# A fused attention and feed-forward kernel on one core: tile 0's late layernorm on ScalarE, mask work on GpSimd in pieces, and phi_q@KV of four tiles in pairs

## The chip, the core and the metric

The kernel runs on one core of a Trainium2 chip. The core has TensorE (PE in the profile: matmuls, and PEld, its weight loads), VectorE (DVE), ScalarE (ACT), GpSimd (POOL) and SyncE (SP, which here only issues DMAs), each with a queue of its own that it works through in order; they wait for each other through semaphores. Matmuls write to PSUM, which has eight banks. The metric is the device time of one execution in microseconds; times below are microseconds unless marked otherwise.

## What is computed

For one sequence of 2048 rows of 640 numbers, all in bf16:

```
x  = A_x;  n = layernorm(x)
q, k, v = split(n @ wqkv)                       # 32 heads of 20
pq, pk = q @ w_phi[h], k @ w_phi[h]             # per head, 20 x 20
phi_q = [softmax(pq), softmax(-pq)]             # over the 20; phi_k alike
kv = phi_k^T @ v;  z = sum over rows of phi_k   # per head
h  = x + (phi_q @ kv / (phi_q . z + 1e-6)) @ wo
m  = layernorm(h)
out = h + (gelu(m @ w_gate) * (m @ w_up)) @ w_down     # 1536 inner
```

## The kernel before

The 2048 rows are 16 tiles of 128 rows (t = 0 to 15), four of them a block (b = 0 to 3). The 640 columns are five chunks of 128. The order of every engine's queue is the order in which the code issues instructions (`manual_schedule`), written out by hand.

**First stage, lines 411 to 505.** For each tile: layernorm statistics, the normalized tile transposed into `LN1T` (by PE for tiles 0 to 5, by a transposing DMA on SP's queue for the rest), v and k by matmul (k with w_phi folded into the weights), `E` = exp of k with both signs on ACT (L310), their sums per head `sk` on DVE (L317), reciprocals `rs` (L321), and `vt` = v times `rs` for both signs (L325): sign 1 always on POOL, sign 0 on POOL for the tiles in `VP` (0, 2, 4, 6, 9, 11) and on DVE for the others, where it is issued one tile later, between `sk` and `rs` of the next tile. `kv_tile` (L343) sums phi_k^T v of all tiles in one PSUM tile, `kvp`; the last tiles run at the end of the stage, after the first chunks of q. Tiles 0 and 1 go through k and v without their row scale, which is applied later, so their true layernorm must be written into `LN1T` before block 0's q: at t == 10 DVE applies it to tile 0 (`ln_ap(0)`, L144) and to tile 1 (`ln_a(1)`, L390), and SP transposes both. At t == 9, POOL clears `KV` and makes the 0/1 mask `kmask` (two memsets, four affine_selects, two copies into `KV`, L489 to L497). At t == 13 SP issues the loads of `Wg`, `Wo` and `Wu`.

**q.** Chunks of phi_q are numbered 5 b + c, and `QG` groups them in the order in which they run; the first four groups run at t == 15, the rest in the list at lines 739 to 781, with the attention of tiles 0 and 1 between them.

**Second stage: attention of a tile, and the feed-forward.** `attn_a` computes phi_q@KV (`ab`, L546: 20 matmuls on half the rows of the array each) and copies it to `AB` in SBUF; `attn_b` takes denominators on POOL (`pr`, `den`), `attn_b2` their reciprocal `rd` on DVE and the weights `w` on POOL, `attn_b3` the products `tt` and the sum `o` on DVE and a DMA transpose into `oT`; `attn_c` multiplies by wo (`po`); `attn_d` adds x on DVE with the row sum as a by-product (L633, L636); `attn_d2` takes the sum of squares on ACT (`sq`) and five or six tiny POOL instructions (L651 to L657) for the scale; `attn_e` applies the layernorm on ACT (`ln`, L139) and transposes it by DMA into `LN2T`. The feed-forward has units: `gate_up` (`gu`: ten matmuls into two halves, gelu `g` on ACT, product `GT` on DVE) for each of 12 inner chunks f, and `down` (`pd`: 12 matmuls for half of a tile's columns, then `y` on DVE and a store). `weave` runs a list of units and issues, ahead of unit i, the attention steps numbered up to i:

```
weave(gus(0, 0, 256) + downs(0, (0, 1)), ...)      # tiles 0, 1: 16 units
weave(gus(0, 256, 512) + downs(0, (2, 3)), ...)    # tiles 2, 3: 16 units
weave(gus(1, 0, 512) + downs(1, range(4)), ...)    # block 1, then 2 and 3
```

A step's number is that of its tile plus an offset from a tuple (`SHORT`, `SHORT2`, `LONG`), and steps beyond the list's end go over to the next one. Up to `split()`, PSUM is four tiles of two banks (`gtile`), where a gelu waits for both halves of its `gu`; after it, eight single banks (`bank`), where it waits for its own half. `attn_a` copies a tile's `ab` with two ACT copies; `attn_pair`, only after the split, runs two tiles' `ab` back to back into eight banks and gives half of the eight copies to ACT and half to DVE (L559). In before, tiles 8 and 9, 10 and 11, 12 and 13, 14 and 15 are pairs; tiles 2 to 7 are singles.

Of the kernel before, what the change touches and what calls it, by code (L numbers as in the profile page):

```python
# [10 lines left out]
ALU = mybir.AluOpType  # L11
# [6 lines left out]
def kernel(  # L18
# [12 lines left out]
    nc = tc.nc  # L31
# [17 lines left out]
    LQ = (7, 8, 9, 9, 10)  # L49
    FQ = (10, 11, 12, 13, 14)  # L50

    QG = ((0, 1), (2, 3), (4, 5), (6,), (7, 8), (9, 10), (11, 12), (13, 14), (15,), (16,), (17,), (18,), (19,))
    QT = (15, 15, 15, 15)
    T3 = 3

# [20 lines left out]
    x_sb = [const.tile([P, 4, D], BF16, name=f"x_sb{b}") for b in range(NB)]  # L76
# [5 lines left out]

    Eq = [const.tile([P, len(g), 2, 512], BF16, name=f"Eq{j}") for j, g in enumerate(QG)]
    ident = const.tile([P, P], BF16, name="ident")
# [6 lines left out]
    def eq(t, c, s):  # L91
        for E, g in zip(Eq, QG):
            if t // 4 * NC + c in g:
                return E[:, g.index(t // 4 * NC + c), s, t % 4 * P:(t % 4 + 1) * P]

    def small(pool, shape, name, bufs=3):
        return pool.tile(shape, F32, name=name, bufs=bufs)

    def gtile(name):
        return psG.tile([P, 2, 512], F32, name=name, tag="G")  # L100

    def ln_stats(pool, tiles, tag, act=True, between=None, log=False):

        n = len(tiles)
        mv = small(pool, [P, n, nc.vector.BN_AGGR_DIM], "mv" + tag)
        stats = small(pool, [P, n, 2, nc.vector.BN_STATS_DIM], "stats" + tag)
        for j, xt in enumerate(tiles):
            for i in range(2):
                nc.vector.bn_stats(stats[:, j, i, :], xt[:, i * HD:(i + 1) * HD])
                if between and i == j == 0:  # L110
                    between()
        for j in range(n):
            nc.vector.bn_aggr(mv[:, j, :], stats[:, j])
        ve = small(pool, [P, n], "ve" + tag)
        rstd = small(pool, [P, n], "rstd" + tag)
        if log is not False:

            def root():
                nc.scalar.activation(ve, mv[:, :, 1], ACTF.Ln, bias=eps)
                nc.scalar.activation(rstd, ve, ACTF.Exp, scale=-0.5)  # L120

            if log is True:
                root()
            else:
                log.append(root)
        else:
            nc.gpsimd.tensor_scalar_add(ve, mv[:, :, 1], EPS)
            nc.gpsimd.tensor_tensor(rstd, ve, nhalf[:, 0:n], op=ALU.pow)

        mr = small(pool, [P, n], "mr" + tag)  # L130
        if act:
            for j in range(n):
                nc.gpsimd.tensor_scalar(mr[:, j:j + 1], mv[:, j, 0:1], rstd[:, j:j + 1], -1.0,
                                        op0=ALU.mult, op1=ALU.mult)
        return [(xt, mv[:, j, 0:1], rstd[:, j:j + 1], mr[:, j:j + 1]) for j, xt in enumerate(tiles)]
# [11 lines left out]
    def transpose_to(dst, src, on_pe, on_dve=False):  # L147

        if on_pe:
            tp = psG.tile([P, 16, P], BF16, name="tp", tag="G")  # L150
            for c in range(NC):
                nc.tensor.transpose(tp[:, c, :], src[:, c * P:(c + 1) * P], ident)  # L152
            (nc.vector.tensor_copy if on_dve else nc.scalar.copy)(dst, tp[:, 0:NC, :])  # L153
        else:
            nc.sync.dma_start_transpose(dst, src)
# [7 lines left out]
    p1 = p1_cm.__enter__()  # L163
# [81 lines left out]
    lnp, Ek, Vt = {}, {}, {}  # L245

    CT = (0, 1)
    nrstd = [p1.tile([P, 1], F32, name=f"nrstd{t}") for t in CT]

    def ln_0(t):  # L250
        xt, mean, rstd, _ = lnp[t] = ln_stats(p1, [x_sb[0][:, t, :]], f"c{t}", False, None, True)[0]
        nc.gpsimd.tensor_scalar(nrstd[t], rstd, -1.0, None, op0=ALU.mult)
        xc = fp.tile([P, D], BF16, name="xc", bufs=2)
        nc.vector.tensor_scalar(xc, xt, mean, None, op0=ALU.subtract)
        return xc
# [5 lines left out]
    def ln_ap(t, on_act=False, on_pe=False):  # L261
        ln = (ln_act if on_act else ln_dve)(p1, "1", *lnp[t])
        if on_pe:
            lnp[t] = ln
        else:
            transpose_to(LN1T[t // 4][:, :, t % 4 * P:(t % 4 + 1) * P], ln, False)
# [92 lines left out]
    def q_mm(j, part=(0, 1)):  # L359

        if 0 in part:
            pqs[j] = gtile("pq")
        for i, bc in enumerate(QG[j]):
            if i not in part:
                continue
            b, c = divmod(bc, NC)
            for kc in range(NC):
                nc.tensor.matmul(pqs[j][:, i, :], lhsT=Wq2[:, kc, c * P:(c + 1) * P], rhs=LN1T[b][:, kc, :],  # L368
                                 start=(kc == 0), stop=(kc == NC - 1))

    def q_exp(j, signs=(0, 1)):
        for s in signs:
            nc.scalar.activation(Eq[j][:, :, s, :], pqs[j][:, 0:len(QG[j])], ACTF.Exp, scale=(1.0, -1.0)[s])  # L373

# [82 lines left out]
    for t in range(NT):  # L457
        if t == T3:
            ps_cm.close()
            psG = ps_cm.enter_context(tc.tile_pool(name="psG", bufs=3, space=PSUM, reuse_waits="tile"))  # L460
            psK = ps_cm.enter_context(tc.tile_pool(name="psK", bufs=1, space=PSUM, reuse_waits="tile"))
            kvp = psK.tile([P, 2, 512], F32, name="kvp")
        k_tile(t)
        if t == 0:
            ln_ap(6)
        if t in FQ:
            fold(WqT, Wq2, True, [i for i, f in enumerate(FQ) if f == t])
        for j in range(len(QT)):
            if t == QT[j]:
                q_mm(j)  # L470
                q_exp(j)
        for i in KVG.get(t, ()):
            kv_tile(i)
        if 0 < t < NT - 4:
            v_mm(t + 4)
        if t > 0 and t + 6 < NT:
            ln_ap(t + 6, on_act=True)
        if 0 < t < NT - 4:
            v_ev(t + 4)
        if t % 2 == 0 and t + 8 < NT:  # L480
            ln_st(t + 8, t + 9)
        k_norm(t)
        load_T(WqT, 0, *[i for i, f in enumerate(LQ) if f == t])
        if t == 10:

            ln_ap(0)
            transpose_to(LN1T[0][:, :, P:2 * P], ln_a(1), False)
        if t == 9:
            nc.gpsimd.memset(KV, 0.0)  # L489
            nc.gpsimd.memset(kmask, 1.0)  # L490
            for r in HALF:
                nc.gpsimd.affine_select(out=kmask[r], in_=kmask[r], pattern=[[4, NC], [-Dh, 4]],
                                        compare_op=ALU.is_ge, fill=0.0, base=0, channel_multiplier=1)
                nc.gpsimd.affine_select(out=kmask[r], in_=kmask[r], pattern=[[-4, NC], [Dh, 4]],
                                        compare_op=ALU.is_ge, fill=0.0, base=Dh - 1, channel_multiplier=-1)
            nc.gpsimd.tensor_copy(KV[:, :, 0, :, KC - 1], kmask)
            nc.gpsimd.tensor_copy(KV[:, :, 1, :, 0], kmask)  # L497
        if t == 13:
            nc.sync.dma_start(Wg, wg_v)
            nc.sync.dma_start(Wo, wo_v)  # L500
            nc.sync.dma_start(Wu, wu_v)
# [60 lines left out]
    def attn_a(t, dve=0):  # L562
        attn_a_mm(t)
        AB, ab = ABs[t % 2], st[t, "ab"]
        for u in ((1, 0) if t in (5,) else (0, 1)):
            (nc.vector.tensor_copy if u >= 2 - dve else nc.scalar.copy)(
                AB[:, :, u * UH:(u + 1) * UH].rearrange("p s h f -> p s (h f)"), ab[u][:, :, 0:UH * KC])
        st[t] = AB
# [215 lines left out]
    def attn_at(t, i, offs):  # L784

        fns = (attn_a, attn_b, attn_b2, attn_b3, attn_c, attn_d, attn_d2, attn_e)
        return [(i + o, fn, t) for fn, o in zip(fns, offs) if o >= 0]

    SHORT = (0, 2, 3, 4, 9, 9, 10, 12)
    SHORT2 = (0, 2, 3, 4, 10, 10, 11, 13)  # L790
    LONG = (0, 1, 2, 5, 5, 6, 7)

    def attn_rest(t, i):
        return [(i + o, fn, t) for fn, o in zip((attn_b, attn_b2, attn_b3, attn_c, attn_d, attn_d2, attn_e), LONG)]

    weave(gus(0, 0, 256) + downs(0, (0, 1)),
          attn_at(2, 0, (-1, 0, 1, 2, 7, 7, 8, 10)) + attn_at(3, 1, (1, 2, 3, 4, 9, 9, 10, 12)) + attn_at(4, 6, SHORT2) + attn_at(5, 9, SHORT2) +
          attn_at(6, 13, SHORT2))  # L800
    weave(gus(0, 256, 512) + downs(0, (2, 3)),
          attn_at(7, 0, SHORT) + [(12, split), (14, attn_pair, 8), (16, attn_pair, 10)] + attn_rest(8, 15) +
          attn_rest(9, 17) + attn_rest(10, 19) + attn_rest(11, 21))
    weave(gus(1, 0, 512) + downs(1, range(4)),
          [(18, attn_pair, 12), (20, attn_pair, 14)] + attn_rest(12, 19) + attn_rest(13, 21) + attn_rest(14, 23) +
# [34 lines left out]
```

## Time and profile before

| what | before |
|---|---|
| time, median of 3 runs (lowest, highest) | 277.28 (276.76, 277.5) |
| the profiled execution's own time | 277.27 |
| its span, first to last instruction | 275.5 |
| PE busy in the span | 270.3 |
| granted TensorE clock | 1.000 |

The span by stages, with each engine's busy time (from the view that sums busy time in windows):

| stage | window | PE | DVE | ACT | POOL |
|---|---|---|---|---|---|
| start | 0 to 16.5 | 14.90 | 11.24 | 10.90 | 5.32 |
| k, v, first part | 16.5 to 46 | 29.50 | 28.99 | 27.10 | 24.95 |
| k, v, second part, first q | 46 to 70.2 | 23.49 | 22.34 | 18.55 | 15.69 |
| q, tiles 0 and 1 | 70.2 to 89.5 | 19.30 | 13.39 | 15.73 | 2.49 |
| first weave | 89.5 to 116.9 | 27.36 | 18.84 | 15.29 | 10.93 |
| second weave | 116.9 to 142.7 | 25.80 | 15.87 | 14.06 | 10.96 |
| the rest | 142.7 to 275.5 | 129.93 | 65.03 | 38.56 | 26.77 |

How to read it: PE's busy time fills nearly all of every stage after the start. A row of the profile's time order gives start, duration, engine, line of the code, operation, output and inputs with their shapes; "xN" merges N instructions, and brackets give the idle time before and what ended it. An instruction that waits inside the engine for something else than a semaphore shows this as a longer duration, not as idle time.

### The profile page before, as it was taken

The numbers are of one execution on the slowest core, as the hardware profiler recorded it, in microseconds if no ns is written. First come the engines' busy times: TensorE is split into PE (matmuls) and PEld (weight loads), VectorE is DVE, ScalarE is ACT, GpSimd is POOL, SyncE is SP. The second block draws the span as 40 slices with busy tenths as digits, with TensorE's granted clock in tenths as the row PEclk, the third lists the DMA queues.
The fourth block names the chain that finished last, engine by engine and source line by source line (L and its number), as shares of the span: only waits on it lengthen the run. The fifth ranks groups of instructions, "written<-read, shape, count | busy, mean of one in ns | idle before, by whom it ended". The sixth has DMA issues, their size and how long they took to land.

```text
span 275.5 us, 5939 instructions
## 1 busy us (share of the span) xinstructions
PE 270.3 (98%) x2345; PEld 173.6 (63%) x2345; DVE 175.7 (64%) x333; ACT 140.2 (51%) x241; POOL 97.1 (35%) x218
## 2 busy tenths in 40 slices
PE   7999999999899999999999999999999999999995
PEld 4777777765455887788764545675455576444574
DVE  5889999999495776675478773356866333333322
ACT  5789898869489755374552345223245510223100
POOL 4248897765202317365312553101165300000000
DMA  7963525589820021323111142110123111000011
GB/s 197 209 230 61 75 51 101 83 266 394 264 91 0 4 48 38 84 48 77 26 48 48 26 69 51 38 61 2 48 47 71 27 48 50 24 0 0 0 50 48
DMA packets 42235, 21.37 MB, mean 78 GB/s; under 512 B 35040, under 2 KB 40416, under 8 KB 42208
## 3 DMA queue, kind: packets, MB, share of 16 engines
q1 hardware_dynamic: 41552, 20.98, 30.1%
q8 instruction: 18, 0.29, 0.5%
q10 hardware_dynamic: 656, 0.03, 0.2%
q14 instruction: 9, 0.07, 0.1%
HBM read 10.18 MB, written 2.62 MB: 46 GB/s over the span
## 4 chain that ended last, share of the span: by engine, by line
PE 86%; issue 4%; DVE 4%; DMA 2%; ACT 1%; POOL 1%; SPq 0%; DVEq 0%; ACTq 0%; POOLq 0%
PE gu L678 37%; PE pd L697 19%; PE po L618 8%; PE pv L277 6%; PE pk L277 5%; PE pq L368 5%; PE ab L546 2%; DMA Wv<-in_A_wqkv_dram 2%; DVE sk L317 2%; DVE rs L321 1%; PE kvp L343 1%; PE tp L152 1%; POOL vt L325 1%; PE pv L293 1%; PE wa L232 1%
## 5 line engine op out<-in xcount | busy, mean ns | idle before, releaser
L681 ACT ACTIVATE g<-gu 128x512 bf16<-128x512 f32 (+1 forms) x60 | 30.7, 512 | 68.9 <-PE gu L678 68.7
L684 DVE TENSOR_TENSOR GT<-gu,g 128x512 bf16<-128x512 f32 (+1 forms) x60 | 34.5, 580 | 47.8 <-PE gu L678 39.2
L678 PE MATMUL gu<-LN2T,Wg 128*128 128x512 bf16 (+1 forms) x300 | 61.8, 337 | 0.0
L678 PE MATMUL gu<-LN2T,Wu 128*128 128x512 bf16 (+1 forms) x300 | 61.8, 337 | 0.0
L697 PE MATMUL pd<-Wd,GT 128*128 128x320 bf16 (+2 forms) x396 | 53.5, 295 | 0.0
L697 PEld LDWEIGHTS <-GT 128*128 128x128 bf16 x396 | 37.9, 98 | 14.7 <-DVE GT L684 0.2
L678 PEld LDWEIGHTS <-Wu 128*128 128x128 bf16 x300 | 29.4, 98 | 22.6
L678 PEld LDWEIGHTS <-Wg 128*128 128x128 bf16 x300 | 28.8, 98 | 21.4
L277 PEld LDWEIGHTS <-LN1T 128*128 128x128 bf16 x290 | 27.8, 98 | 10.5
L700 DVE TENSOR_TENSOR y<-pd,x_sb 128x320 bf16<-128x320 f32 (+2 forms) x29 | 13.9, 480 | 28.9 <-PE pd L697 28.9
L325 POOL TENSOR_TENSOR vt<-vS,rs 128x672 bf16<-128x672 bf16 x22 | 29.1, 1343 | 9.1 <-DVE rs L321 8.8
L618 PE MATMUL po<-Wo,oT 128*128 128x320 bf16 x160 | 24.3, 299 | 0.0
L277 PE MATMUL pk<-Wk,LN1T 128*128 128x320 bf16 x160 | 24.2, 299 | 0.0
L368 PE MATMUL pq<-LN1T,Wq 128*128 128x512 bf16 x100 | 23.1, 379 | 0.0
L317 DVE TENSOR_REDUCE sk<-E 128x64 f32<-128x1280 bf16 x16 | 22.9, 1430 | 0.0
L373 ACT ACTIVATE Eq<-pq 128x1024 bf16<-128x1024 f32 (+1 forms) x26 | 20.0, 830 | 1.7 <-PE pq L368 1.7
L618 PEld LDWEIGHTS <-oT 128*128 128x128 bf16 x160 | 15.6, 98 | 7.4 <-ACT oT L153 0.5
L310 ACT ACTIVATE E<-pk 128x640 bf16<-128x640 f32 x28 | 18.2, 707 | 3.8 <-PE pk L277 3.8
L277 PE MATMUL pv<-Wv,LN1T 128*128 128x320 bf16 x130 | 19.8, 299 | 0.0
L595 DVE TENSOR_TENSOR tt<-AB,w 128x1280 bf16<-128x1280 f32 x12 | 17.8, 1486 | 1.1 <-POOL w L588 0.9
L139 ACT ACTIVATE ln<-x_sb,v,rstd 128x640 bf16<-128x640 bf16 x14 | 12.9, 920 | 10.4 <-POOL v L657 10.0
L368 PEld LDWEIGHTS <-Wq 128*128 128x128 bf16 x100 | 9.4, 98 | 10.0
(114 smaller groups left out, 292.8 us busy)
## 6 DMA issues: line engine op xcount, KB each, us to landing
out_dram<-y SPq DMA_DIRECT2D x15, 160.0 KB, 1.8
Wg<-in_B_w_gate_dram SPq DMA_DIRECT2D x1, 1920.0 KB, 7.9
Wu<-in_B_w_up_dram SPq DMA_DIRECT2D x1, 1920.0 KB, 12.8
Wd<-in_B_w_down_dram SPq DMA_DIRECT2D x1, 1920.0 KB, 7.9
x_sb<-in_A_x_dram SPq DMA_DIRECT2D x2, 640.0 KB, 6.3
Wo<-in_A_wo_dram SPq DMA_DIRECT2D x1, 800.0 KB, 9.5
x_sb<-in_A_x_dram SPq DMA_DIRECT2D x4, 160.0 KB, 3.4
Wv<-in_A_wqkv_dram SPq DMA_DIRECT2D x2, 320.0 KB, 4.6
```

The costliest lines, as they stand in the source:

```text
L277: nc.tensor.matmul(ps[:, u, 0:HD], lhsT=lnT(t, c), rhs=W[:, c, u * HD:(u + 1) * HD], start=(c == 0), stop=(c == NC - 1))
L310: nc.scalar.activation(Ek[t][:, s, :].rearrange("p (u f) -> p u f", u=2), pk[:, :, 0:HD], ACTF.Exp, scale=((lnp[t][2], nrstd[t]) if t in C ...
L317: nc.vector.reduce_sum(sk, Ek[t].rearrange("p s (h f) -> p (s h) f", f=Dh), axis=AX.X)
L325: eng.tensor_tensor(vt[:, s], vS[t % 8], rs[:, s * H:(s + 1) * H, None].to_broadcast([P, H, VC]), ALU.mult)
L368: nc.tensor.matmul(pqs[j][:, i, :], lhsT=Wq2[:, kc, c * P:(c + 1) * P], rhs=LN1T[b][:, kc, :], start=(kc == 0), stop=(kc == NC - 1))
L373: nc.scalar.activation(Eq[j][:, :, s, :], pqs[j][:, 0:len(QG[j])], ACTF.Exp, scale=(1.0, -1.0)[s])
L595: nc.vector.tensor_tensor(tt.rearrange("p s (h f) -> p s h f", f=Dh), num, w[:, :, :, None].to_broadcast([P, 2, H, Dh]), ALU.mult)
L618: nc.tensor.matmul(pos[u], lhsT=st[t][:, c, :], rhs=Wo[:, c, u * HD:(u + 1) * HD], start=(c == 0), stop=(c == NC - 1))
L678: nc.tensor.matmul(gu[i][:, 0:n], lhsT=W[:, c, f * P:(f + 1) * P], rhs=LN2T[b][:, c, a0:a1], start=(c == 0), stop=(c == NC - 1))
L681: nc.scalar.activation(g[:, 0:n], gu[0][:, 0:n], ACTF.Gelu_apprx_tanh)
L684: nc.vector.tensor_tensor(st[b, "g", f][:, a0:a1], gu[1][:, 0:n], g[:, 0:n], ALU.mult)
L697: nc.tensor.matmul(ps, lhsT=st[b, "g", f][:, tl * P:(tl + 1) * P], rhs=Wd[:, f, f0:f1], start=(f == 0), stop=(f == NF - 1))
```

## The change

- `ln_ap(0)`, tile 0's late layernorm, goes from DVE at t == 10 to ACT at t == 12, ahead of E of tile 13 in ACT's queue; its transpose is issued behind that of tile 1. ACT's form needs minus mean times scale, so `ln_0` computes that for tile 0 with one more POOL instruction. Tile 1's (`ln_a(1)`) stays.
- POOL's mask work is cut in three: the memsets at t == 7, the affine_selects at t == 8, the copies into `KV` at t == 10, each behind that tile's `vt`.
- `QG`: chunks 5 and 6 (block 1) run first; 4 stands alone.
- Tile 3's steps move (offsets below); tile 4 to 7's `ab` become two pairs in the down units of the first weave, ahead of units 13 and 15, and `split()` moves from unit 12 of the second weave to unit 12 of the first. The other steps of tiles 4 to 7 follow at new offsets (`MID`), most of them in the second weave, and now use single banks (two L633 per tile in place of one L636, one more POOL instruction, L651).

Lines of the changed kernel are up to four higher (L678 becomes L682, L559 becomes L563).

```
-    QG = ((0, 1), (2, 3), (4, 5), (6,), (7, 8), ...
+    QG = ((5, 6), (0, 1), (2, 3), (4,), (7, 8), ...
...
-        xt, mean, rstd, _ = lnp[t] = ln_stats(...)[0]
+        xt, mean, rstd, mr = lnp[t] = ln_stats(...)[0]
         nc.gpsimd.tensor_scalar(nrstd[t], rstd, -1.0, None, op0=ALU.mult)
+        if t == 0:
+            nc.gpsimd.tensor_scalar(mr, mean, nrstd[0], None, op0=ALU.mult)
...
         if t == 10:
-
-            ln_ap(0)
             transpose_to(LN1T[0][:, :, P:2 * P], ln_a(1), False)
-        if t == 9:
+        if t == 12:
+            ln_ap(0, on_act=True)
+        if t == 7:
             nc.gpsimd.memset(KV, 0.0)
             nc.gpsimd.memset(kmask, 1.0)
+        if t == 8:
             for r in HALF:
                 nc.gpsimd.affine_select(out=kmask[r], ...)
                 nc.gpsimd.affine_select(out=kmask[r], ...)
+        if t == 10:
             nc.gpsimd.tensor_copy(KV[:, :, 0, :, KC - 1], kmask)
             nc.gpsimd.tensor_copy(KV[:, :, 1, :, 0], kmask)
...
-        for u in ((1, 0) if t in (5,) else (0, 1)):
+        for u in ((1, 0) if t in (4,) else (0, 1)):
...
-    SHORT = (0, 2, 3, 4, 9, 9, 10, 12)
-    SHORT2 = (0, 2, 3, 4, 10, 10, 11, 13)
+    MID = (0, 1, 2, 8, 8, 9, 11)
     LONG = (0, 1, 2, 5, 5, 6, 7)
-    def attn_rest(t, i):
-        return [(i + o, fn, t) for fn, o in zip((attn_b, attn_b2, attn_b3, attn_c, attn_d, attn_d2, attn_e), LONG)]
+    def attn_rest(t, i, offs=LONG):
+        return [(i + o, fn, t) for fn, o in zip((attn_b, attn_b2, attn_b3, attn_c, attn_d, attn_d2, attn_e), offs)]
...
     weave(gus(0, 0, 256) + downs(0, (0, 1)),
-          attn_at(2, 0, (-1, 0, 1, 2, 7, 7, 8, 10)) + attn_at(3, 1, (1, 2, 3, 4, 9, 9, 10, 12)) + attn_at(4, 6, SHORT2) + attn_at(5, 9, SHORT2) +
-          attn_at(6, 13, SHORT2))
+          attn_at(2, 0, (-1, 0, 1, 2, 7, 7, 8, 10)) + attn_at(3, 1, (2, 2, 3, 4, 8, 8, 9, 11)) +
+          [(12, split), (13, attn_pair, 4), (15, attn_pair, 6)] + attn_rest(4, 14, MID) + attn_rest(5, 16, MID) +
+          attn_rest(6, 18, MID) + attn_rest(7, 20, (0, 1, 2, 7, 7, 8, 10)))
     weave(gus(0, 256, 512) + downs(0, (2, 3)),
-          attn_at(7, 0, SHORT) + [(12, split), (14, attn_pair, 8), (16, attn_pair, 10)] + attn_rest(8, 15) +
+          [(14, attn_pair, 8), (16, attn_pair, 10)] + attn_rest(8, 15) +
           attn_rest(9, 17) + attn_rest(10, 19) + attn_rest(11, 21))
```

More of the change, by code (lines that the diff above doesn't have):

```diff
@@ L50 @@
     FQ = (10, 11, 12, 13, 14)
-    QG = ((0, 1), (2, 3), (4, 5), (6,), (7, 8), (9, 10), (11, 12), (13, 14), (15,), (16,), (17,), (18,), (19,))
+    QG = ((5, 6), (0, 1), (2, 3), (4,), (7, 8), (9, 10), (11, 12), (13, 14), (15,), (16,), (17,), (18,), (19,))
     QT = (15, 15, 15, 15)
@@ L250, in ln_0 @@
     def ln_0(t):
-        xt, mean, rstd, _ = lnp[t] = ln_stats(p1, [x_sb[0][:, t, :]], f"c{t}", False, None, True)[0]
+        xt, mean, rstd, mr = lnp[t] = ln_stats(p1, [x_sb[0][:, t, :]], f"c{t}", False, None, True)[0]
         nc.gpsimd.tensor_scalar(nrstd[t], rstd, -1.0, None, op0=ALU.mult)
+        if t == 0:
+            nc.gpsimd.tensor_scalar(mr, mean, nrstd[0], None, op0=ALU.mult)
         xc = fp.tile([P, D], BF16, name="xc", bufs=2)
```

## The prediction

> **What bounds the kernel now.** I read the page's header and busy times first, then the waits of PE, then the time order of each engine where PE waits or where the change touches it. All times are microseconds on the profile's clock.
>
> ```profile
> span 275.5 us, 5939 instructions
> PE 270.3 (98%) x2345; PEld 173.6 (63%) x2345; DVE 175.7 (64%) x333; ACT 140.2 (51%) x241; POOL 97.1 (35%) x218
> ```
> ```profile
> PE wu L214 <- PEq L824: 0.8, 1, 0.8
> PE kvp L343 <- POOL vt L325: 0.7, 1, 0.7
> PE pv L293 <- DMA Wv<-in_A_wqkv_dram: 0.5, 1, 0.5
> ```
> PE is busy 98% of the span at full clock, and its waits sum to 2.0. A gain must shorten PE's work or remove the one wait in the middle (kvp, at 69.87; the matmul before it started at 68.96, and 20 ns is the step there, so removing it gives at most 0.88). A loss is any new wait on PE, and there are many places for one.
>
> That wait ends a chain of DVE and POOL work from 46 on. The time order of DVE, then of POOL (start, duration):
> ```profile
> 51.53 1.81 DVE L144 TENSOR_SCALAR ln<-x_sb,mvc,rstdc 128x640 bf16<-128x640 bf16 x1
> 53.27 0.43 DVE L390 TENSOR_SCALAR ln<-x_sb,va 128x640 bf16<-128x640 bf16 x1
> 53.62 1.47 DVE L317 TENSOR_REDUCE sk<-E 128x64 f32<-128x1280 bf16 x1
> 55.01 1.72 DVE L325 TENSOR_TENSOR vt<-vS,rs 128x672 bf16<-128x672 bf16 x1
> ```
> ```profile
> 49.76 2.58 POOL L325 TENSOR_TENSOR vt<-vS,rs 128x672 bf16<-128x672 bf16 x2 [1.32 <-DVE rs L321]
> 52.28 0.83 POOL L489 MEMSET KV<- 128x880 bf16 x1
> ...
> 54.70 1.31 POOL L325 TENSOR_TENSOR vt<-vS,rs 128x672 bf16<-128x672 bf16 x1
> ```
> Tile 0's ln needs 0.43 (its neighbour's duration) and took 1.81: it ended 0.23 after POOL's memset. DVE's vt ended 0.72 after POOL's vt (56.01). So an elementwise instruction of DVE stands while POOL works, and here it stood through two POOL instructions in a row, vt and memset.
>
> **Part 1: ln(0) to ScalarE, mask work in pieces.** DVE loses L144. The other ln (tile 1, L390) stays in its place and is asked for at the same 51.53. POOL's vt of tile 9 still runs to 52.34; behind it now comes vt of tile 10 at once (its rs ended at 51.61), to 53.6. If DVE stands through both, as it did through vt and memset, L390 ends at 53.85 to 54.2, after the two small copies, and sk(11) starts 0.15 to 0.5 later than 53.62. But vt(10) of DVE then finds POOL idle: 0.85 instead of 1.72, the uncovered duration at 67.79. rs(11) comes 0.4 to 0.75 earlier than 56.65. The four mask instructions, now ahead of vt(9), can take 0.5 of that back. If DVE gets in after one POOL instruction, L390 ends at 52.6, rs(11) comes 2.0 earlier, and the whole 0.88 is gained. If the memset, now behind vt(7) of POOL, holds up DVE's vt(7), DVE loses 0.83 there and the stage ends up to 0.5 later. From rs(11) on both orders are equal. Between −0.5 and 0.88 I take a gain of **0.4**, the middle of the case that the row shows.
>
> The Trainium skill ("SBUF — State Buffer", Who interferes with whom) says that a DVE instruction with two SBUF inputs contends with GpSimd instructions that read SBUF, not with one that only writes, and that the lock goes to whoever issues first, for the whole instruction. By its first half the memset costs vt(7) nothing; by its second DVE should get in between two POOL instructions, the gain would be 0.88 and the sum 278.24. The row of 1.81 speaks against the second half.
>
> On ACT ln(0) costs 0.92 at 54.40; E(13) behind it ends at 56.4, and ACT was idle for 1.43 before 57.75, so PE's pk and wa find their banks free. Its transpose on SP starts near 55.4 and lands 2.6 later, at 58.0; Wg, Wo and Wu behind it are issued about 1 later and needed after 79. Chunks of block 0, which need it, come second (61.4) since chunks 5, 6 go first. The added product for tile 0 runs on POOL at 5.7, idle until 8.29. All this costs nothing; without the chunk order the margin would be 1.2 (59.23 against 58.0).
>
> **Part 2: pairs.** The chain of waits gives the price of phi_q@KV on PE:
> ```profile
> 97.48 0.50 PE ab L546 x20
> 97.97 1.20 PE gu L678 x10
> ...
> 137.49 0.94 PE ab L546 x40
> 138.42 3.37 PE pd L697 x24
> ```
> A single costs 0.50 and 0.11 in what follows (10 gu matmuls elsewhere take 1.09); a pair 0.94 and 0.11 (24 pd: 3.26). Four singles become two pairs: 4 x 0.61 − 2 x 1.05 = **0.34 saved**.
>
> The price is in the covers. I put the changed order on the old clock from tile 2's ab (89.56), with a gu unit at 1.09, a po at 1.36, a pd unit at 1.63. Without ab(4) in front, po(2) comes at 98.39 (was 99.01) and po(3) at 101.93 (was 104.25); their oT lands 2.6 after issue, at 98.45 and about 102.1. Waits: 0.1 and 0.15. Pair (4,5) starts near 108.4, and ACT's copies of it stand behind ln(3). Two views of the old pair (8,9) show how tight that is:
> ```profile
> 134.06 3.42 PE L697 MATMUL pd<-Wd,GT 128*128 128x320 bf16 x24
> 137.42 1.00 PE L546 MATMUL ab<-KV,Eq 64*128 64x88 bf16 x40
> 138.35 3.43 PE L697 MATMUL pd<-Wd,GT 128*128 128x320 bf16 x24
> ```
> ```profile
> 135.53 0.92 ACT L139 ACTIVATE ln<-x_sb,v,rstd 128x640 bf16<-128x640 bf16 x1 [0.82 <-POOL v L657]
> 137.82 1.52 ACT L559 COPY AB<-ab 128x352 f32<-128x352 f32 x4 [1.38 <-PE ab L546]
> ```
> The pair takes all eight PSUM banks; the next pd uses the bank that ACT's first copy frees, at 138.27, only 0.08 ahead. A later ACT is a later PE, one for one. For pair (4,5), ln(3) ends at about 109.1 where the copy wanted 108.8: 0.2. These three: **0.45 lost** (bounds 0 and 0.6).
>
> Then tiles 4 to 7 run their whole tail inside gus(0, 256, 512). Pair (6,7) starts at 112.50. DVE copies its half and reaches rd(4) 2.24 later (old: 141.72 to 143.96), 114.74, and tt(4) at 115.7. Steps from the old rows: tt to o 1.52, o to GT 0.41, GT to rd 0.36, rd to tt 0.95, together 3.24. So tt(5) 118.94, tt(6) 122.18, then o, GT, rd, GT (0.27), 0.36 and the two L633 of tile 4 (0.81): tt(7) at 125.91. DVE is saturated; po(4) was done at 123.09. Now POOL's statistics of tile 4 meet tt(7):
> ```profile
> 106.74 1.44 POOL L652 TENSOR_SCALAR v<-sm 128x1 f32<-128x1 f32 x1 [0.92 <-DVE x_sb L636]
> 108.26 0.38 POOL L653 TENSOR_SCALAR v<-v 128x1 f32<-128x1 f32 x1
> ```
> That is the same meeting in before (tt 106.55 to 108.04): 0.27 became 1.44, and the last of five POOL steps ended 3.47 after tt began, ln at 3.50. With one more step (L651, 0.29), ln(4) is at 129.70. ACT's order is ln(4), sq(5), ln(5), sq(6), ln(6), ln(7), copies of pair (8,9). ln to the next takes 0.83, sq to its ln 2.32 (1.00 to L654, then 0.35, 0.66, 0.27, 0.04): sq(5) 130.53, ln(5) 132.85, sq(6) 133.68, ln(6) 136.00. Tile 7's six POOL steps (2.28) wait for tile 6's: ln(7) 138.36, first copy 139.19. PE's sum from 112.50 (0.94, 1.74, twelve gu, four po, two pd) puts pair (8,9) at 136.97, so the copy is due at 137.37. It is 1.82 late, less 0.08: **1.74 lost**. Upward, POOL's pr may hold up each tt (0.13 three times: 2.1); downward, an undelayed ACT costs 0.
>
> PE finds its banks otherwise: the closest are po(5) (GT freed at 125.1, due 125.9), po(6) (128.2, 128.8) and tile 7's oT (130.5, 131.2). Queued behind ACT's wait are those copies, GT of unit 11 for the last pd matmul (0.2, inside the 1.74), and nothing on SP that is due. LN2T(7) lands near 142 and is due at 143.
>
> **Sum,** against the profiled execution's own 277.27 (span 275.5 and 1.77 around it; the median of the runs is 277.28): 277.27 − 0.40 − 0.34 + 0.45 + 1.74 = 278.72. Forecast **278.7**.
>
> **Rivals.** (a) Faster: the covers hold. If ln(7) starts by 136.5, ACT meets the copy, nothing is lost, and 277.27 − 0.88 − 0.34 = 276.05. For it: in before ACT idled 1.38 ahead of that copy, and tiles 8 to 11 go through the same order unharmed. Against: their units last 2.16, these 1.09, and DVE needs 4.4 per tile (3.24, a GT, two L633) where PE gives 3.5 (two gu, one po). It decides where the ln chain is 1.74 shorter. (b) No change: DVE and POOL do not meet at tt(7). Then sq(5) follows STT(5) at 129.4 and the copy is 0.65 late: 277.27 − 0.40 − 0.34 + 0.45 + 0.65 = 277.6. Likewise if (a)'s cover holds but Part 1 brings little: 277.0. (c) Worse: DVE falls 0.4 further behind, PE waits for GT too, and Part 1 turns into 0.5: 277.27 + 0.5 − 0.34 + 0.6 + 2.1 = 280.1. (d) Part 1 does not do what it says, since L390 now waits as long as both did: the 0.40 goes, 279.1, inside the forecast's range.
>
> **How the numbers follow.** Forecast with (d), 278.1 to 279.5: 0.50. (b), 276.5 to 278.1: 0.27. (a): 0.15. (c): 0.08. The range leaves out about half of (a) and most of (c): 276.2 to 279.8; the forecast's own is 278.1 to 279.5. A measurement of this kernel tells about 0.3% (0.83) from no change: faster (below 276.44) 0.15, same 0.28, slower (above 278.11) 0.57.
>
> **What would show it.** Right (lines of the changed kernel): PE waits for ACT's copy of pair (8,9) by 1 to 2; ACT's ln of tile 7 ends after that pair has started; POOL's L655 or L656 of tile 4 is over 1 long beside tt(7); kvp's wait is 0 to 0.6; DVE's L392 over 1.5 long. Wrong: pd follows that pair at once (then (a) or (b)), or gu waits for DVE inside the wave (then (c)). L392 at 0.5 to 1.0 would mean that DVE does get in between POOL's instructions.

## The result, and the profile after

The changed kernel takes 278.15 (277.92 to 278.49, six executions) against 277.02 for before (276.59 to 277.50, six): a ratio of 1.0037 with a 95% interval of 1.0024 to 1.0051, so 1.0 slower. Header, busy times and PE's waits of the changed kernel (in the last view: engine, line, what released it, then total, number and longest wait):

```profile
span 276.5 us, 5955 instructions
PE 270.0 (98%) x2332; PEld 174.0 (63%) x2345; DVE 177.9 (64%) x350; ACT 138.6 (50%) x242; POOL 98.2 (35%) x223
```
```profile
PE po L622 <- DVE x_sb L637: 1.5, 1, 1.5
PE wu L214 <- PEq L828: 0.8, 1, 0.8
PE pv L295 <- DMA Wv<-in_A_wqkv_dram: 0.2, 1, 0.2
PE pd L701 <- ACT AB L563: 0.2, 1, 0.2
```

The wait at kvp is gone and two new ones have come. The time order of PE shows where:

```profile
130.18 0.71 PE L682 MATMUL gu<-LN2T,Wu 128*128 128x256 bf16 x5
132.36 1.53 PE L622 MATMUL po<-Wo,oT 128*128 128x320 bf16 x10 [1.48 <-DVE x_sb L637]
...
138.18 1.00 PE L550 MATMUL ab<-KV,Eq 64*128 64x88 bf16 x40
139.34 3.42 PE L701 MATMUL pd<-Wd,GT 128*128 128x320 bf16 x24 [0.16 <-ACT AB L563]
```

Po of tile 7 was due at 130.72 (130.18 and half a gu unit, 0.54) and came 1.64 late; pd behind the pair of tiles 8 and 9 came 1.16 after its start in place of 0.94, so 0.22 late (139.12 was due). The stretch from ab of tile 2 to block 1's first gu took 53.10 before (89.56 to 142.66) and takes 54.86 now (88.77 to 143.63), 1.76 more. Three gaps in the first weave (0.10 and 0.12 at po of tiles 2 and 3, 0.11 at pd behind the pair of tiles 4 and 5) and the two of the tail make 2.19; so the other 0.43 is what the pairs save, taken as what is left over.

**Why po of tile 7 stands.** The waits of PE name x_sb of tile 6, and its first half did end at 132.34, 0.02 ahead of po. But that list is inferred from what ended last. The order of PEld, the weight loads, gives another releaser (idle time and releaser in brackets):

```profile
130.07 0.54 PEld L682 LDWEIGHTS <-Wu 128*128 128x128 bf16 x5
132.36 0.66 PEld L622 LDWEIGHTS <-oT 128*128 128x128 bf16 x6 [1.75 <-DMA oT<-o]
```

Po's first matmul needs that weight load, and by the program's semaphores the load waits for the transposing DMA of tile 7's o, while the matmul waits for x_sb of tile 5, done at 129.2, not of tile 6 (po's second half also needs GT of unit 8, done at 129.5). The same wait stands in act_copies below, whose trace settles it: there po started at 131.85, while the first half of x_sb of tile 6 was still running (131.74 to 132.22). The DMA asked by its line, from 126 to 129:

```profile
L155 SPq DMA_TRANSPOSE oT<-o x1: 1202/1202/1202, 127.8 to 127.8; - x1
...
  PEld L622: 1.8, 1
...
DMA to landing us min/median/max: 4.5/4.5/4.5
```

Issued at 127.79, landed 4.5 later, near 132.3; the transpose of tile 6 took 2.6. At 2.6 it would have landed at 130.4, ahead of 130.72. The DMA view of 129.7 to 131.2 (busy share of the 16 DMA engines in 40 slices, then packets, megabytes and share by queue) shows what was there:

```profile
DMA  8739000000000000000000000000000000100000
...
q1 hardware_dynamic: 92, 0.02, 6.7%
q8 instruction: 1, 0.02, 4.6%
```

The transpose is nearly through when one 16 KB packet of an instruction queue starts (129.82, 1.11 long). For 1.0 nothing else moves; then come the last seven packets of the transpose (130.92 to 131.10). Its end is told 1.2 after them, where tile 6's came 0.5 after its last packet; what lies in the rest, no row shows.

**Why pd stands behind the pair.** This is the chain of the forecast. POOL, then ACT:

```profile
125.87 1.38 POOL L655 TENSOR_TENSOR sm<-sm 128x1 f32<-128x1 f32 x1 [0.61 <-DVE x_sb L637]
127.35 0.51 POOL L656 TENSOR_SCALAR v<-sm 128x1 f32<-128x1 f32 x1
```
```profile
129.58 0.92 ACT L139 ACTIVATE ln<-x_sb,v,rstd 128x640 bf16<-128x640 bf16 x1 [2.31 <-POOL v L661]
...
132.70 0.92 ACT L139 ACTIVATE ln<-x_sb,v,rstd 128x640 bf16<-128x640 bf16 x1 [0.94 <-POOL v L661]
...
138.03 0.92 ACT L139 ACTIVATE ln<-x_sb,v,rstd 128x640 bf16<-128x640 bf16 x1 [1.28 <-POOL v L661]
138.86 1.49 ACT L563 COPY AB<-ab 128x352 f32<-128x352 f32 x4
```

Two of POOL's steps for tile 4 stand beside tt of tile 7 (1.38 for 0.19, 0.51 for 0.27), ln of tile 4 waits 2.31 for them, ln of tile 7 comes 8.45 after that of tile 4, and ACT's first copy (0.45 long) frees its bank only at 139.31. Without the stop at po, and with ACT where it is, pd would have been due at 139.12 − 1.64 = 137.48 and would have waited 1.83. So the two latenesses lie one inside the other: PE's stop at po hides all but 0.22 of ACT's. Together they cost 1.86, not 1.64 + 1.83.

### The profile page after: what moved, and what is told of

It is laid out like the page before. It is cut to its first block, busy times and chain, and to the rows that moved or that the text cites. A ratio compares the mean times of both kernels' runs of the same rounds, so it can differ in the third digit from the quotient of the medians.

```text
span 276.5 us, 5955 instructions
## 1 busy us (share of the span) xinstructions
PE 270.0 (98%) x2332; PEld 174.0 (63%) x2345; DVE 177.9 (64%) x350; ACT 138.6 (50%) x242; POOL 98.2 (35%) x223
## 4 chain that ended last, share of the span: by engine, by line
PE 90%; ACT 3%; POOL 2%; DMA 2%; issue 2%; DVE 1%; SPq 0%; POOLq 0%; ACTq 0%
PE gu L682 36%; PE pd L701 17%; PE pk L279 8%; PE pq L370 8%; PE po L622 7%; PE pv L279 7%; PE kvp L345 2%; PE ab L550 2%; DMA Wv<-in_A_wqkv_dram 2%; PE wa L232 1%; ACT ln L139 1%; POOL rstd L660 1%; PE tp L152 1%; ACT sq L652 1%; PE pv L295 1%
## 5 line engine op out<-in xcount | busy, mean ns | idle before, releaser
L682 PE MATMUL gu<-LN2T,Wg 128*128 128x512 bf16 (+1 forms) x291 | 61.3, 335 | 0.5
L682 PE MATMUL gu<-LN2T,Wu 128*128 128x512 bf16 (+1 forms) x300 | 61.8, 336 | 0.0
L682 PEld LDWEIGHTS <-Wu 128*128 128x128 bf16 x300 | 29.3, 98 | 22.6
L682 PEld LDWEIGHTS <-Wg 128*128 128x128 bf16 x300 | 29.0, 98 | 21.3
L704 DVE TENSOR_TENSOR y<-pd,x_sb 128x320 bf16<-128x320 f32 (+2 forms) x33 | 15.9, 481 | 32.2 <-PE pd L701 32.2
L599 DVE TENSOR_TENSOR tt<-AB,w 128x1280 bf16<-128x1280 f32 x10 | 15.2, 1516 | 0.9 <-POOL w L592 0.6
```

What stands on the lines that cost most here:

```text
L682: nc.tensor.matmul(gu[i][:, 0:n], lhsT=W[:, c, f * P:(f + 1) * P], rhs=LN2T[b][:, c, a0:a1], start=(c == 0), stop=(c == NC - 1))
L704: nc.vector.tensor_tensor(y[:, f0:f1], ps, x_sb[b][:, tl, f0:f1], ALU.add)
```

## Experiments

Each variant was timed in five rounds beside before (5 to 12 executions); the ratio is to before, with its 95% interval. "oT(7)" is the time from issue to landing of the transpose of tile 7's o; "stretch" is the time from ab of tile 2 to block 1's first gu in the profiled execution (53.10 before), free of what happens earlier.

| kernel | median | ratio | interval | PE's waits at po of tile 7, at the pair's pd, at block 1's gu | oT(7) | stretch |
|---|---|---|---|---|---|---|
| changed | 278.15 | 1.0037 | 1.0024 to 1.0051 | 1.48, 0.16, 0 | 4.5 | 54.86 |
| part1_only | 276.82 | 0.9992 | 0.9978 to 1.0007 | as before, none |  | 53.10 |
| part2_only | 278.76 | 1.0067 | 1.0043 to 1.0091 | 0.98, 0.66, 0 | 4.0 | 54.86 |
| mask_only | 277.04 | 1.0003 | 0.9988 to 1.0018 | as before, none |  | 53.11 |
| ln_only | 276.85 | 0.9997 | 0.9985 to 1.0009 | as before, none |  | 53.10 |
| tt7_pieces | 278.16 | 1.0039 | 1.0022 to 1.0057 | 1.30, 0, 0 | 4.2 | 54.51 |
| later_ln | 278.98 | 1.0070 | 1.0050 to 1.0090 | 1.07, 0, 0.84 | 4.1 | 55.20 |
| act_copies | 278.24 | 1.0044 | 1.0025 to 1.0062 | 0.93, 0.56, 0 | 4.1 | 54.71 |
| both_tail | 278.72 | 1.0068 | 1.0046 to 1.0090 | 1.32, 0, 0.72 | 4.5 | 55.35 |
| load_shift | 280.06 | 1.0113 | 1.0095 to 1.0131 | 0, 0, 0.75 | 2.6 | 54.07 |
| early_tt | 276.99 | 1.0001 | 0.9990 to 1.0012 | 0, 0.50, 0 | 4.1 | 53.55 |
| early_tt_w1 | 277.05 | 1.0007 | 0.9996 to 1.0019 | 0, 0.50, 0 | 4.1 | 53.59 |
| early_tt_swap | 276.98 | 1.0008 | 0.9986 to 1.0030 | 0, 0.49, 0 | 4.1 | 53.56 |

### The two parts, each alone

**part1_only** is before with the first half of the diff (`QG`, `ln_0`, ln of tile 0, the mask work).

> Before with Part 1 alone (ln of tile 0 on ACT, mask work in pieces, chunks 5 and 6 first). Theory A (the changed kernel's trace, where PE's wait at kvp is gone and the first weave starts 0.79 earlier): 0.8 to 0.9 faster than before, kvp wait 0, about 276.1. Rival (the size in the prediction): 0.4 faster, a kvp wait of 0.4 left, 276.6.

Measured: no kvp wait, and yet no gain that is clear of noise: 0.9992, an interval from 0.6 faster to 0.2 slower. The 0.8 is excluded, the rival's 0.4 is not. **part2_only** is the changed kernel with that half undone.

> The changed kernel with Part 1 undone, so that only the pairs and the new offsets of tiles 3 to 7 are left. Theory A: the two parts add up; pairs save 0.4, the first weave loses 0.3, the tail of tiles 4 to 7 loses 1.9, so 1.8 slower than before, 278.8, with the wait of po for x_sb near 1.5 as in the changed kernel. Rival: the loss in the tail comes from Part 1 having moved the weave 0.8 ahead of something fixed (a transfer); then the tail loses only about 1.0 here and the time is near 278.0.

Measured: 1.0067, slower by 1.9, as theory A says, with three executions at 278.1 to 278.4 and three at 279.1 to 279.7. But its trace holds the answer to part1_only: up to 72 it runs the same program as before, and it has no kvp wait. Before, then part2_only:

```profile
66.87 2.29 PE L343 MATMUL kvp<-vt,E 128*64 128x84 bf16 x110
69.87 0.38 PE L343 MATMUL kvp<-vt,E 128*64 128x84 bf16 x10 [0.71 <-POOL vt L325]
```
```profile
66.90 2.68 PE L343 MATMUL kvp<-vt,E 128*64 128x84 bf16 x120
```

All 120 matmuls run through, where before's last ten stand. Set side by side, the two traces agree to 0.1 on PE until then, and every DVE and POOL instruction from 16 to 70 is 0.68 to 0.70 later in before. The difference begins at one DVE row; before, then part2_only:

```profile
16.47 0.89 DVE L109 BATCH_NORM_STATS2 stats<-x_sb 128x6 f32<-128x320 bf16 x2 [0.62 <-DMA x_sb<-in_A_x_dram]
```
```profile
15.79 0.88 DVE L109 BATCH_NORM_STATS2 stats<-x_sb 128x6 f32<-128x320 bf16 x2
```

A load of x landed 4.9 after its issue in before's profiled execution and 4.0 in the other. In the four traces without the whole of Part 1 (mask_only and ln_only follow below), the kvp wait is there when x is late and not otherwise. The time of before does vary: 52 of its 89 executions took 276.32 to 276.98, the other 37 took 277.09 to 279.01. That x makes this spread is not shown; early_tt_swap (below) has Part 1, and 3 of its 12 executions still took 278.0 to 278.3 where the others took 276.8 to 277.3.

### The halves of Part 1

```
 mask_only (before with)                 ln_only (before with)
-        if t == 9:                      -            ln_ap(0)
+        if t == 7:                      +        if t == 12:
...                                      +            ln_ap(0, on_act=True)
+        if t == 8:                      ...
...                                      +  mr of tile 0, QG with (5, 6) in front
+        if t == 10:
```

> Before with only the mask work in pieces; both late ln stay on DVE, the chunk order is the old one. Theory A (a TENSOR_SCALAR of DVE gets in between two vt of POOL, but not between vt and the memset behind it; what cost DVE its time in before was the memset): L144 takes 1.4 and L390 at most 1.3, vt of tile 10 is then beside an idle POOL, and the kvp wait is 0 to 0.1: 0.8 faster, 276.2. Rival (ln of tile 0 on DVE is what made DVE late): L144 and L390 both stand, 0.0 to 0.4 faster, kvp wait 0.4 or more.

> Before with ln of tile 0 on ACT and chunks 5 and 6 first, the mask work uncut at t == 9. Theory A (the memset keeps the TENSOR_SCALAR out): L390 stands through vt and memset, about 1.8, only the 0.43 of one ln is gained, kvp wait 0.4 to 0.5, 276.6. Rival (DVE gets in after any POOL instruction): L390 takes 1.0, the whole 0.88 is gained, kvp wait 0.

DVE's rows, mask_only and then ln_only:

```profile
52.09 1.42 DVE L144 TENSOR_SCALAR ln<-x_sb,mvc,rstdc 128x640 bf16<-128x640 bf16 x1
53.42 1.43 DVE L390 TENSOR_SCALAR ln<-x_sb,va 128x640 bf16<-128x640 bf16 x1
```
```profile
50.97 1.81 DVE L392 TENSOR_SCALAR ln<-x_sb,va 128x640 bf16<-128x640 bf16 x1
```

The durations are theory A's (1.4 between three vt of POOL, 1.8 with the memset behind the vt); the times are not. In mask_only x was late (DVE waited 0.69) and a kvp wait of 0.37 is left; in ln_only x was in time and there is none. Neither differs from before in the time. What Part 1 does in full can be read from traces with a late x: DVE waited 0.75 for it in both_tail, 1.28 in early_tt and 1.18 in early_tt_w1, all with Part 1, and kvp waits in none. It takes a wait out of some executions, not 0.9 out of each. That a late x is the cause was read from these traces; a kernel that makes x late on purpose was not tried.

How much that is on average, the table suggests when its times are set against its stretches, which do not contain Part 1. In all nine kernels with the whole of Part 1, load_shift aside, the time exceeds before's by 0.2 to 0.7 less than the stretch does (the changed kernel 1.0 against 1.76, early_tt 0.0 against 0.45, part1_only −0.2 against 0). In the three without it, or with half of it, the two agree within 0.1 (part2_only 1.9 against 1.76). Taken singly most of these differences lie within the noise of the times (0.3 to 0.6), so a gain near the 0.4 of the forecast is likely and not shown.

### The tail of tiles 4 to 7

Four edits of the changed kernel:

```
 tt7_pieces: attn_b3, tile 7            tt in four instructions of eight heads
 later_ln:   MID (.., 9, 11)         -> (.., 10, 12);  tile 7's e: 10 -> 11
 act_copies: attn_pair, t == 6          all eight AB copies on ACT
 both_tail:  later_ln and act_copies
```

> The changed kernel with tt of tile 7 cut into four instructions of eight heads. Theory A (the loss starts where POOL's statistics of tile 4 stand through tt of tile 7, 1.38 and 0.51 for 0.19 and 0.27): POOL gets in after one piece, L655 of tile 4 takes 0.5 or less, ln of tile 4 comes 0.8 to 1.0 earlier, PE's wait at po falls from 1.5 to 0.5, about 277.3. Rival L (DVE's lag alone: x_sb of tile 4 is 2.3 behind po whatever POOL does): nothing changes, 278.1, or a little slower by the three added instructions.

> The changed kernel with the steps d2 and e of tiles 4 to 6 one unit later (MID ends in 10, 12) and e of tile 7 one unit later, behind the pair of tiles 8 and 9. Theory A (the loss is the place of ln and sq in ACT's queue, ahead of gelus that are ready): the gelu of unit 9 runs at 128.3 in place of 131.1, GT and x_sb of tile 6 follow, PE waits neither at po nor at the pair's copies, 1.4 to 1.7 faster than the changed kernel, about 276.6; what may be left is 0 to 0.3 at block 1's first gu, for LN2T of tile 7. Rival L (DVE has more work per tile than PE gives it time for, so it stays late however ACT is ordered): at most 0.4 faster, 277.8.

> The changed kernel with all eight AB copies of tiles 6 and 7 on ACT, which is idle there until 115.4. Theory A and rival L agree that DVE's chain starts 1.7 earlier, tt of tile 4 at 113.6. A: PE's wait at po goes, since ln of tile 4 ends near 128.7, and 0.3 to 0.6 are left at the copies of tiles 8 and 9, about 276.9. L: the 1.7 is given back whole, 276.4. If gu of units 1 and 2 finds its banks late, a wait of 0.5 to 1 appears at 115 instead and the time stays near 278.

> The changed kernel with both: d2 and e later, and the copies of tiles 6 and 7 on ACT. Theory A: no wait is left in the second weave, 1.9 faster than the changed kernel, 276.2 to 276.4, that is 0.7 faster than before. Rival L: 277 or more, because PE still meets a late DVE.

No gain in any. In tt7_pieces POOL's first step for tile 4 fell to 0.38, but each of the next steps stood beside the next piece (0.70, 0.34, 0.47), and ln of tile 4 came only about 0.45 earlier. In later_ln the gelu did run at 128.1 and x_sb of tile 6 at 129.75, done at 130.6; still po waited 1.07, and ln of tile 7, now behind the pair's copies, made the first gu of block 1 wait 0.84. In act_copies DVE won nothing: y of the last down unit, queued ahead of tt of tile 4, held it idle for 1.92 (tt at 115.28). And po started while x_sb of tile 6 was running. Act_copies' PEld, then its PE:

```profile
131.84 1.20 PEld L622 LDWEIGHTS <-oT 128*128 128x128 bf16 x10 [1.21 <-DMA oT<-o]
```
```profile
131.85 1.53 PE L622 MATMUL po<-Wo,oT 128*128 128x320 bf16 x10 [0.93 <-DVE GT L688]
```

Theory A as I had put it, that x_sb of tile 6 behind gelu, sq and ln keeps po, falls by later_ln and act_copies; rival L falls by later_ln, where DVE was idle from 130.66 to 131.49. The list of waits now names a GT of a later unit than the one that po needs by the program. Common to all four is the transpose, 4.1 to 4.5 where 2.6 is normal. And the two stops trade: part2_only, whose tail is the changed kernel's, has 0.98 + 0.66 where that has 1.48 + 0.16, both 1.64, with a transpose of 4.0 and 4.5. So the load was moved next:

```
 load_shift (both_tail with)
-    warm(*[512] * 7, *[P] * 8)
+    warm(*[512] * 7, *[P] * 8, *[2] * 20)
```

> both_tail with twenty more tiny warm-up matmuls at the very start of PE's queue, 40 instructions with their weight loads; nothing else is changed. In all five kernels with the pairs, one 16 KB packet of the instruction queue starts at 128.9 to 130.2 and the transpose of tile 7's o, in flight then, lands 4.1 to 4.5 after its issue in place of 2.6. Theory D (that load is PE's own, comes every 256 of its instructions and holds up the transpose, which po of tile 7 waits for): the load moves some 2 earlier, to 127.3, the transpose lands after 2.6, the wait of 1.3 at po goes, and the time is 1.0 to 1.3 less than both_tail's, about 277.5; 0.7 is left at block 1's first gu. Rival L (the transpose is late for another reason, or po waits for DVE): the wait stays at 1.3, 278.7.

```profile
130.93 1.53 PE L622 MATMUL po<-Wo,oT 128*128 128x320 bf16 x10
133.39 1.52 PE L622 MATMUL po<-Wo,oT 128*128 128x320 bf16 x10
```
```profile
PE pv L279 <- DMA LN1T<-ln: 2.2, 2, 1.2
PE wu L214 <- PEq L828: 0.8, 1, 0.8
PE gu L682 <- DMA LN2T<-ln: 0.8, 1, 0.8
```

The wait at po of tile 7 is gone (only gu's 1.09 lies between 130.93 and 133.39), and its transpose landed after 2.6: the place is theory D's. The total is not: all loads moved, and two of them now hold up transposes of LN1T in the first stage (landed after 4.2 and 4.4), for which PE waits 2.2. The load near 129 came nearly 4 earlier against po of tile 6, not 2, and hit tile 6's transpose (4.4), which cost po of tile 6 only some 0.2. So the load is what kept po in both_tail, and the stretch shortens by 1.28. For the changed kernel the same is read from its packets and its 4.5, not from a run of its own. The changed kernel itself with the load moved was not tried; an estimate from the rows above is that PE would then wait about 1.8 at pd instead.

The other way is to make ACT's chain earlier:

```
 early_tt (act_copies with)        tile 4's b3: offset 2 -> 1
 early_tt_w1 (early_tt with)       c, d, d2, e of tile 2 one unit later,
                                   of tile 3 one (e 1.5) later
 early_tt_swap (early_tt with)     at t == 8, attn_pair's engines exchanged
```

> The changed kernel with the eight AB copies of tiles 6 and 7 on ACT and tt of tile 4 one unit earlier, ahead of y of the last down unit, which had kept DVE idle for 1.9 in act_copies. Theory D: DVE's chain is 1.7 earlier, so the transpose of tile 7's o is issued near 125.2 and has landed before the load at 129.5; x_sb of tile 4 is done at 123.3 and ln of tile 4 at 128, so the gelu of unit 9 is no longer kept; po of tile 7 does not wait, ln of tile 7 ends before the copies of the pair are due: 1.5 faster than the changed kernel, 276.6. Rival A without the load (only ACT's order counts): the same place is cured, 276.6 as well. Rival S (DVE is saturated and gives nothing back): the wait at po stays over 1, 278.

> early_tt, with po of tiles 2 and 3 one unit later and ln of tile 3 behind ACT's copies of the pair of tiles 4 and 5. If the three small waits of the first weave (0.10 at po of tile 2, 0.12 at po of tile 3, 0.11 at pd behind the pair) are what the trace says, 0.3 faster than early_tt, 276.3. Rival: LN2T of tile 3 becomes late for the second weave's first gu, a wait of 0.5 or more there, 276.9.

> early_tt, with the copies of the pair of tiles 8 and 9 dealt the other way round: DVE takes the banks that ACT took, the first one among them. In early_tt the one wait left in the second weave is 0.50 at pd behind this pair, because the first bank waits for ACT, which is behind ln of tile 7 until 137.75, while DVE is free at 137.24. If that is so, pd follows the pair at once, and the time is 0.4 to 0.5 less: 276.5, 0.3 to 0.5 less than before. Rival: y of the last down unit or the second bank keeps pd, the wait stays, and the time is early_tt's, 277.0.

Early_tt's PE waits, and the po and pd rows:

```profile
PE wu L214 <- PEq L828: 0.8, 1, 0.8
PE pd L701 <- ACT AB L563: 0.5, 1, 0.5
PE pv L279 <- DMA LN1T<-ln: 0.3, 1, 0.3
```
```profile
130.92 1.52 PE L622 MATMUL po<-Wo,oT 128*128 128x320 bf16 x10
133.37 3.42 PE L701 MATMUL pd<-Wd,GT 128*128 128x320 bf16 x24
136.73 1.00 PE L550 MATMUL ab<-KV,Eq 64*128 64x88 bf16 x40
138.23 3.42 PE L701 MATMUL pd<-Wd,GT 128*128 128x320 bf16 x24 [0.50 <-ACT AB L563]
```

With tt of tile 4 at 113.71 the transpose of tile 7 is issued 1.1 earlier (126.67). It still meets the load (4.1), but lands at 130.80, ahead of po at 130.92: no wait. ACT's ln of tiles 4 and 7 come 1.11 earlier too, at 128.47 and 136.92, as far apart as in the changed kernel (8.45): PE's stop at po was not what kept ACT. What is left of ACT's lateness now shows at pd (1.50 from the pair's start where 0.94 is due, 0.56 late). The stretch is 53.55, 1.31 less than the changed kernel's, and the time is that of before (1.0001 in place of 1.0037), although the stretch is still 0.45 longer than before's. Early_tt_w1 removed the three small gaps and put others in their place (0.20 for GT at the first pd); no gain. In early_tt_swap the wait is unchanged, a miss: with the engines exchanged, the pool of banks gave pd the bank of ACT's first copy again. No version here beats before clear of noise.

## Why the prediction was right or wrong, point by point

- **Forecast.** 278.7 for a measured 278.15, slower by 0.4% where 0.5% was forecast. The sign and the main term are right; the reason given for Part 1's term failed, and the place of the tail's. Of the 0.57 between forecast and median, 0.25 is the base: 277.27 was one of the slower executions of before, whose median over six is 277.02.
- **Part 1, 0.40 gained: the reason failed, the size is open.** "The sum is made against its own time" took the kvp wait of one execution for a property of the kernel. In the two profiled executions the whole wait went (the first weave starts 0.79 earlier, although PE of the changed kernel was 0.11 later just ahead of kvp), but there x was late in one and in time in the other. Part 1 alone gave no gain clear of noise (0.6 faster to 0.2 slower); 0.40 lies inside that, and times against stretches speak for 0.2 to 0.7. That the size fits would be luck: a wait of up to 0.9 in some executions is not a saving of 0.4 in each. "The row of 1.81 speaks against the second half" failed too: between two vt DVE does get in. L392 took 1.42, not over 1.5: it came 0.07 behind the start of POOL's second vt, stood through that one alone and was done ahead of the third. With a late x it took 1.42 as well (early_tt). Without Part 1 the measured terms (0.43 saved, 0.33 and 1.86 lost) give 1.76; part2_only took 1.9 more than before.
- **Pairs, 0.34 saved:** 0.43, as what is left over of the stretch.
- **First weave, 0.45 lost:** 0.33; the three places are right, pd behind the pair 0.11 where 0.2 was taken.
- **Tail, 1.74 lost:** 1.86. The chain is right step by step: from the start of the pair of tiles 6 and 7, tt of tile 7 was forecast at 13.4 and ln of tiles 4 and 7 at 17.2 and 25.9; they came at 13.7, 17.5 and 26.0. But only 0.22 was paid where the forecast put it. The step that failed is "tile 7's oT (130.5, 131.2)": it took 2.6 from the neighbouring rows, which by the measured issue leaves a margin of 0.33; the transpose took 4.5, and the margin became a wait of 1.64. The size came out nearly right because ACT's lateness, forecast right (1.83 by the rows for 1.74), lies behind that stop and swallows it. That the stop at po, which the forecast did not have, came out smaller than ACT's lateness is luck.
- **The rule of "SBUF — State Buffer", Who interferes with whom,** of the Trainium skill: its first half holds here (in the changed kernel DVE's vt of tile 7, two inputs, ended at 45.84 while POOL's memset ran from 45.06 to 45.89). Its second half, as the forecast read it, holds between two vt (1.42) and not between vt and memset (1.81 in before, part2_only and ln_only).
- **Rivals.** (b) needed DVE and POOL not to meet at tt of tile 7; they met, 1.38 and 0.51. (a) is refuted by the waits. (c)'s sign, gu waiting for DVE inside the wave, did not come. (d)'s reason, that L390 waits as long as both did, did not come: it took 1.42, where the two had taken 1.81 and 0.43.

## What to carry to other kernels

Before a wait in one profiled execution is priced as a gain, look whether other executions of the same program have it: here the execution with it had a load that landed 0.9 later. Where two latenesses lie one behind the other, the first stop hides the second, so removing one alone moves the wait and not the end; and the releaser that a list of waits names has to be checked against the weight loads, the program's semaphores or a variant in which it was done earlier. An order written by hand ties transposes to places in the instruction stream; moving work also moves it against the instruction loads.

## What the runs showed of the hardware that was not expected

In the fourteen traces there are 560 transposing DMAs within SBUF, 40 in each. For 74 of them a 16 KB packet of queue q8 was in flight at some time between 0.9 and 2.3 after the issue (bounds chosen from these same traces): all landed late, after 3.0 to 4.8, median 4.1. For 31 others it was an 8 KB packet of q14: 23 landed late, the median of the 31 is 3.2. Of the other 455, 442 landed after 2.6; 13 landed later, after up to 4.5, and no row here shows why. The Trainium skill ("Runtime: NRT & Kernel Launch", Instruction fetch mechanics) says that an engine's instructions are refilled in blocks of 16 KiB through a DMA queue of its own and calls the cost mostly hidden; here PE ran on after the load had started (from 129.82 to 130.72 in the changed kernel), but a transpose in flight came late, and through it PE stood for 1.3 in both_tail. That q8 is PE's queue is supported by load_shift, where 20 more matmuls moved all its loads, and not shown otherwise.

A tensor-scalar instruction of DVE that came while POOL's vt ran ended 0.2 after that vt where another vt followed (1.42 long in nine traces with Part 1 and in mask_only), and the next vt then took 1.39 to 1.40 in place of 1.31; where a memset followed, it ended 0.2 after the memset (1.81 in before, part2_only and ln_only). The two cases differ in more than what follows: the first kind came 0.07 to 0.08 behind the vt's start, the second 0.50. Which of the two decides, no run here shows.
